# Transposes of the next batch in a fused attention and MLP kernel: one piece moved behind the second half of a product, one piece moved to another ring of accumulation banks

## The chip, the cores and the metric

The kernel runs on one core of one Trainium2 chip. The metric is the device time of one execution in microseconds (us). One execution is also profiled. Before the change the median of three runs was 752.65 us (752.6 to 754.64).

The engines in the profile are PE (TensorE, the matmuls), PEld (its loading of weights, which overlaps PE), DVE (VectorE), ACT (ScalarE) and SP (issues the transfers). In this kernel TensorE's results go to accumulation memory (PSUM), kept as two rings of two banks and a group of four. A tile taken from a ring of two must wait until the tile taken two places earlier has been read out. The granted clock is the share of TensorE's full speed that the profile shows as allowed. The chain that ended last is the work followed back from the last instruction, at each step to what released it.

## The reference, cut to what matters

```python
def _attn_ref(x, state):                    # x (8, 8, 512, 64), state (8, 8, 32, 64)
    scores = scale * x @ state^T            # softmax over the 32 states, then @ state
    scores2 = scale * state @ x^T           # softmax over the 512 tokens, then @ x
    ...
def _moe_ref(x, w_in, w_out):               # 4352 tokens, 512 -> 2048 -> 512
    h = x @ w_in
    g = h * (1.0 / (1.0 + np.exp(-1.702 * h)))
    return (g @ w_out).astype(np.float32)
```

Everything is float32. The kernel computes the second product (`g @ w_out`) by Strassen's method: seven products of blocks, with sums around them, in place of eight. While it does so for batch b, it prepares the attention of batch b+1 in between.

## The kernel before

`att_state` transposes the state of a batch, and `att_xT` transposes one of four pieces of its x. Each writes one bank of ring A (`att_ps`), and ScalarE copies the bank out. Four transposes fill the bank of a piece. Ring H (`psH`) serves other products.

```python
    def att_ps(shape, name):
        return psA.tile(shape, FP32, tag="att", name=name)        # ring A: two banks

    def att_state(b):
        ps = att_ps([P, P], f"stT_{b}")
        nc.tensor.transpose(ps, stn[b].rearrange("p g d -> p (g d)"), ident)
        ...
        nc.scalar.copy(A[b]["stT"], ps)

    def att_xT(b, j):
        ...
        ps = att_ps([P, SCH, P], f"xT_{b}_{j}")
        for c in range(SCH):
            nc.tensor.transpose(ps[:, c], x_heads(b, c, j), ident)
        nc.scalar.copy(A[b]["xT"][:, j], ps.rearrange("p c q -> p (c q)"))
```

The seven products call hooks behind each half. "P1a" is behind the first half of the first product, "P1b" behind its second half and "P2a" behind the first half of the second product. In front of the hooks at P1a runs the tail of the previous stage (`rest`: two short products, each with an addition on VectorE and a gelu on ScalarE, and sums on VectorE).

```python
        at("P1a", att_state, b)
        at("P1a", att_xT, b, 0)
        at("P1a", att_xT, b, 1)
        at("P1b", att_xT, b, 2)
        at("P1b", att_xT, b, 3)
        at("P2a", att_scores, b)
        at("P2a", att_M, b, 0)             # ring A
        at("P2a", att_M, b, 1, True)       # ring H
        ...
        hooks["P1a"] = [(rest, ())] + hooks.get("P1a", [])
```

These hooks run for five batches (3 to 7), while batches 2 to 6 are in their seven products.

Of the kernel before, what the change touches and what calls it, by code (L numbers as in the profile page):

```python
# [10 lines left out]
FP32 = mybir.dt.float32  # L11
# [9 lines left out]
def kernel(  # L21
# [36 lines left out]
    P = 128  # L58
# [3 lines left out]
    SCH = S // P  # L62
# [21 lines left out]
    psH = ctx.enter_context(tc.tile_pool(name="psH", bufs=2, space=bass.MemoryType.PSUM))  # L84
# [4 lines left out]
    def att_ps(shape, name):  # L89
        return psA.tile(shape, FP32, tag="att", name=name)  # L90
# [49 lines left out]
    def x_heads(b, c, j):  # L140
        return xn[b][:, c, NG * j : NG * (j + 1)].rearrange("q g d -> q (g d)")
# [111 lines left out]
        A[b]["stT"] = apool.tile([P, P], FP32, tag="stT", name=f"stT_{b}", bufs=2)  # L253
        nc.scalar.copy(A[b]["stT"], ps)

    def att_xT(b, j):
        if j == 0:
            A[b]["xT"] = apool.tile([P, NPR, S], FP32, tag="xT", name=f"xT_{b}")
        ps = att_ps([P, SCH, P], f"xT_{b}_{j}")
        for c in range(SCH):  # L260
            nc.tensor.transpose(ps[:, c], x_heads(b, c, j), ident)  # L261
        nc.scalar.copy(A[b]["xT"][:, j], ps.rearrange("p c q -> p (c q)"))
# [160 lines left out]
    def att_slots(b):  # L423

        slots = [[] for _ in range(14)]

        def at(i, fn, *args):
            slots[i].append((fn, args))

        at(0, att_state, b)  # L430
        for j in range(NPR):
            at(j, att_xT, b, j)

        at(5, att_scores, b)
        at(5, att_M, b, 0)
        at(5, att_M, b, 1, True)
        at(5, att_blocks, b)
        at(5, att_s_max, b)
        at(5, att_s_exp, b)
        at(5, att_x_exp, b)  # L440
        at(5, att_s_norm, b)
        at(5, att_x_norm, b)
        for g in range(NG):
            at(8, att_eT, b, g)
        at(9, att_sread, b)
        at(9, att_M, b, 3, True)
        at(9, att_M, b, 2)
        at(11, att_srT, b)
        sums_of = up_sums(b)
        for i, fn, args in ((10 if k < 5 else 11 if k < 12 else 12, *v) for k, v in enumerate(sums_of)):  # L450
            at(i, fn, *args)
        return slots
# [288 lines left out]
    def hooks_next(b):  # L741

        h = {}

        def at(name, fn, *args):
            h.setdefault(name, []).append((fn, args))

        at("P1a", att_state, b)
        at("P1a", att_xT, b, 0)
        at("P1a", att_xT, b, 1)  # L750
        at("P1b", att_xT, b, 2)
        at("P1b", att_xT, b, 3)
        at("P2a", att_scores, b)
        at("P2a", att_M, b, 0)
        at("P2a", att_M, b, 1, True)
        at("P2a", att_blocks, b)
        at("P2a", att_s_max, b)
        at("P2a", att_s_exp, b)
        for g in range(NG):
            at("P2a", x_max, b, g)  # L760
            at("P2a", x_sub, b, g)
        at("P2a", x_exp, b)
        at("P2", att_s_norm, b)
        for name, fn, *args in (
            ("P6.1", x_sum, 0), ("P6.2", x_sum, 1), ("P6.3", x_inverse), ("P6.4", x_scale, 0), ("P6.6", x_scale, 1),
        ):
            at(name, fn, b, *args)
        for g in range(NG):
            at("P6", att_eT, b, g)
            at("P6", x_back, b, g)  # L770
        at("P4a", att_sread, b)
        at("P4a", att_M, b, 3, True)
        at("P4a", att_M, b, 2)
        steps = up_sums(b)
        for name, n in (("P4b", 5), ("P7.1", 2), ("P7.2", 1), ("P7.3", 1), ("P7.4", 1), ("P7.6", 1), ("P7", 1), ("P3a", 3)):
            for fn, args in steps[:n]:
                at(name, fn, *args)
            steps = steps[n:]
        assert not steps
        at("P3a", att_srT, b)  # L780
        return h


    def up_sums(b):

        a = A[b]

        def tt(out, x0, x1, op=ALU.subtract):
            nc.vector.tensor_tensor(out=out(), in0=x0(), in1=x1(), op=op)

        def rooms(step):
            if step == 0:
                t = apool.tile([P, NG, NB, Ns], FP32, tag="e1", name=f"ta_{b}").rearrange("p g i n -> p (g i n)")
                a["T"] = [t[:, QT * i : QT * (i + 1)] for i in range(4)]
            elif step == 1:
                t = apool.tile([P, NPR, S], FP32, tag="xT", name=f"ms_{b}")
                a["S1"], a["S2"] = t[:, :2], t[:, 2:]
            else:
                t = apool.tile([P, NG, SCH, P], FP32, tag="eT", name=f"m4_{b}")
                a["S4"] = t.rearrange("p g c q -> p g (c q)")  # L800

        def T(i):
            return lambda: a["T"][i]

        def R(g, i):
            return lambda: a["aT"][:, g, QT * i : QT * (i + 1)]

        def M(c, g):
            return lambda: a["M", c][:, g]

        def V(name, c):
            return lambda: a[name][:, c]

        steps = [(rooms, (0,))]
        steps += [(tt, v) for v in ((T(0), R(0, 1), R(0, 0)), (T(1), R(1, 1), T(0)), (T(2), R(1, 1), R(0, 1)), (T(3), R(1, 0), T(1)))]
        steps.append((rooms, (1,)))
        for c in range(2):
            steps.append((tt, (V("S1", c), M(2 + c, 0), M(2 + c, 1), ALU.add)))
            steps.append((tt, (V("S2", c), V("S1", c), M(c, 0))))
            steps.append((tt, (M(2 + c, 0), M(c, 0), M(2 + c, 0))))  # L820
        steps.append((rooms, (2,)))
        steps += [(tt, (V("S4", c), M(c, 1), V("S2", c))) for c in range(2)]
        return steps
# [248 lines left out]
    for b in range(2, B):  # L1072
        rest = up_strassen(b, S, *parts_x(b))
        if b + 1 < B:
            hooks = hooks_next(b + 1)
        else:

            steps, left, right = sr_sums()
            hooks = {"P3a": steps[9:] + [(low_third, (T2,)), (low_third, (T3,))]}
            for k, name in enumerate(("P1b", "P2a", "P2", "P5a", "P5b", "P6", "P4a", "P4b", "P7")):  # L1080
                hooks[name] = [steps[k]]
        hooks["P1a"] = [(rest, ())] + hooks.get("P1a", [])
        strassen_two(b, out_of(b), hooks)
        if b + 2 < B:
            load_state(b + 2)
            load_x(b + 2)
# [35 lines left out]
```

## Time and profile before

| | before |
|---|---|
| median of runs | 752.65 us |
| span of the profiled run | 750.4 us |
| TensorE busy | 731.6 us, 98% |
| VectorE busy | 501.7 us, 67% |
| ScalarE busy | 232.1 us, 31% |
| TensorE waiting for the copy of the state | 5.3 us in 5 waits |
| granted TensorE clock, mean | 0.998 |

TensorE sets the time, so the rows to look for are those in which TensorE itself stands still. The prediction shows them. One more row is VectorE's first work on the scores of the next batch, from the order of time (start us, length us, engine, line, operation, tiles, shapes, count, and in brackets the idle time before it and what ended it):

```profile
337.52 1.31 DVE L292 STREAM_TRANSPOSE e<-o 128x512 f32<-128x512 f32 x2 [3.19 <-PE o L279]
```

VectorE was idle for 3.19 us before it.

### The profile page before, as it was taken

The page shows a single profiled execution, that of the slowest core. Times are in us where ns is not written, and L with a number is a line of the kernel's source. Part 1 is how long each engine was busy: PE and PEld are TensorE (multiplying, and loading weights), DVE is VectorE, ACT ScalarE, POOL GpSimd, SP SyncE. Part 2 cuts the span into 40 slices and gives each one's busy share as a digit, 9 for nine tenths or more (in the row PEclk, how much of TensorE's full clock was granted, in tenths as well). Part 3 has the DMA queues.
Part 4 walks back from the last instruction along what each step waited for, and adds up shares of the span by engine and source line. Part 5 has one row for each costly group of instructions (what it writes and reads, how often), then busy time and mean ns, then how long its engine had stood idle before and what let it go on. Part 6 is the DMA issues. An engine that isn't in the chain of part 4 may idle for free.

```text
span 750.4 us, 10915 instructions
## 1 busy us (share of the span) xinstructions
PE 731.6 (98%) x4555; PEld 567.4 (76%) x4555; DVE 501.7 (67%) x947; ACT 232.1 (31%) x421; POOL 0.8 (0%) x8
## 2 busy tenths in 40 slices
PE   8989999999999999999999999999999999999996
PEld 3433444467888789878888789878887888899995
DVE  5999799615846775567747666677656774768340
ACT  4676511022324511433134322451143313300220
POOL 0000000000000000000000000000000000000000
PEclk9999999999999999999999999999999999999999
DMA  9811245010030000300040003000030001000000
GB/s 236 331 58 56 93 160 144 0 57 1 29 83 5 1 16 29 74 1 15 2 102 1 15 2 93 10 1 16 29 74 1 15 2 42 1 15 29 15 1 28
DMA packets 48768, 35.29 MB, mean 47 GB/s; under 512 B 36432, under 2 KB 44112, under 8 KB 48720
## 3 DMA queue, kind: packets, MB, share of 16 engines
q1 hardware_dynamic: 48720, 34.61, 16.1%
q8 instruction: 35, 0.57, 0.3%
q14 instruction: 13, 0.11, 0.1%
HBM read 25.69 MB, written 8.91 MB: 46 GB/s over the span
## 4 chain that ended last, share of the span: by engine, by line
PE 94%; SPq 2%; ACT 2%; DMA 1%; DVE 1%; issue 0%; DVEq 0%; ACTq 0%
PE o L645 28%; PE o L890 16%; PE o L522 9%; PE h L461 8%; PE o L479 7%; PE low L597 6%; PE upx L890 6%; PE o L597 4%; PE M L279 4%; PE xT L261 1%; SPq L138 1%; PE sr L410 1%; PE o L279 1%; PE upx_sr L890 1%; DMA out_dram<-osb_sr 1%; PE warm L122 1%
## 5 line engine op out<-in xcount | busy, mean ns | idle before, releaser
L900 DVE TENSOR_TENSOR g<-o,g 128x512 f32<-128x512 f32 (+1 forms) x140 | 88.1, 651 | 87.3 <-PE o L890 86.3
L645 PE MATMUL o<-w_out,g 128*128 128x256 f32 x576 | 130.0, 380 | 0.0
L645 PEld LDWEIGHTS o<-w_out,g 128*128 128x128 f32 x576 | 107.4, 190 | 18.1 <-issue 4.2
L897 ACT ACTIVATE g<-g 128x512 f32<-128x512 f32 (+1 forms) x84 | 49.8, 600 | 100.5 <-DVE g L900 100.5
L890 PE MATMUL o<-ta,M 128*128 128x256 f32 x192 | 49.3, 379 | 0.0
L890 PE MATMUL upx<-aT,M 128*128 128x256 f32 x192 | 49.3, 379 | 0.0
L890 PE MATMUL o<-ta,ms 128*128 128x256 f32 x192 | 48.4, 380 | 0.0
L390 ACT COPY M<-M 128x512 f32<-128x512 f32 x64 | 33.2, 596 | 42.5 <-PE M L279 42.5
L645 PE MATMUL o<-sums,g 128*128 128x256 f32 x192 | 43.8, 382 | 0.0
L522 PE MATMUL o<-w_out,g 128*128 128x256 f32 x192 | 42.9, 380 | 0.0
L645 PE MATMUL o<-sums,later 128*128 128x256 f32 x192 | 42.4, 379 | 0.0
L645 PEld LDWEIGHTS o<-sums,g 128*128 128x128 f32 x192 | 35.6, 190 | 8.6 <-issue 4.2
L522 PEld LDWEIGHTS o<-w_out,g 128*128 128x128 f32 x192 | 36.1, 190 | 6.0 <-issue 1.3
L890 PEld LDWEIGHTS o<-ta,ms 128*128 128x128 f32 x192 | 36.4, 190 | 5.2 <-DVE osb L541 0.3
L890 PEld LDWEIGHTS o<-ta,M 128*128 128x128 f32 x192 | 36.5, 190 | 5.0
L645 PEld LDWEIGHTS o<-sums,later 128*128 128x128 f32 x192 | 36.5, 190 | 5.0
L890 PEld LDWEIGHTS upx<-aT,M 128*128 128x128 f32 x192 | 36.5, 190 | 5.0
L502 DVE TENSOR_TENSOR later<-g,g 128x512 f32<-128x512 f32 (+1 forms) x32 | 20.8, 650 | 21.5 <-ACT g L464 21.5
L279 PE MATMUL M<-w_in,stT 64*32 64x512 f32 x512 | 33.2, 594 | 0.2 <-ACT eT L400 0.2
L461 PE MATMUL h<-low,M 128*128 128x512 f32 x64 | 29.8, 600 | 2.1 <-ACT M L390 2.1
L461 PE MATMUL h<-aT,M 128*128 128x512 f32 x64 | 28.7, 599 | 2.3 <-ACT M L390 2.3
L600 DVE TENSOR_TENSOR pu<-low,pu 128x128 f32<-128x128 f32 x12 | 3.5, 291 | 39.6 <-PE low L597 39.6
(172 smaller groups left out, 1136.6 us busy)
## 6 DMA issues: line engine op xcount, KB each, us to landing
later<-in_moe_w_out_dram SPq DMA_DIRECT2D x16, 512.0 KB
xn<-in_x_dram SPq DMA_DIRECT2D x28, 256.0 KB
w_out<-in_moe_w_in_dram SPq DMA_DIRECT2D x12, 512.0 KB
out_dram<-osb SPq DMA_DIRECT2D x20, 256.0 KB
out_dram<-later SPq DMA_DIRECT2D x12, 256.0 KB
later<-in_moe_w_in_dram SPq DMA_DIRECT2D x4, 512.0 KB
sums<-in_x_dram SPq DMA_DIRECT2D x4, 256.0 KB
stn<-in_state_dram SPq DMA_DIRECT2D x16, 32.0 KB
```

The costliest lines, as they stand in the source:

```text
L122: nc.tensor.matmul(ps, zeros[:, :P], zeros, start=True, stop=True)
L279: nc.tensor.matmul(ps[g][st], A[b]["stT"][rows, st], rhs(rows, j), start=True, stop=True)
L390: nc.scalar.copy(m[:, g], ps[g])
L461: nc.tensor.matmul(hps, lhs[i], rhs[i], start=(i == 0), stop=(i == n - 1))
L479: nc.tensor.matmul(ops, G[key, f // 2][:, f % 2, P * r : P * (r + 1)], w_out[:, f], start=(f == 0), stop=(f == NF - 1))
L502: nc.vector.tensor_tensor(out=s1, in0=a21, in1=a22, op=ALU.add)
L522: nc.tensor.matmul(ps[:, r], lhs[f][:, P * r : P * (r + 1)], rhs[:, f], start=(first and r == 0 and f == 0), stop=(f == HF - 1), skip_grou ...
L597: nc.tensor.matmul(ps, lhs[f], rhs[:, f], start=(f == 0), stop=(f == QF - 1))
L645: nc.tensor.matmul(ps[:, r], lhs[f][:, P * r : P * (r + 1)], rhs[:, f], start=(r == 0 and f == 0), stop=(f == HF - 1), skip_group_check=True,)
L890: nc.tensor.matmul(ps[:, k], lhs[i][:, o : o + P], rhs[i], start=(first and k == 0 and i == 0), stop=(i == n - 1), skip_group_check=True,)
L897: nc.scalar.activation(out=dst, in_=src, func=AF.Gelu_apprx_sigmoid)
L900: nc.vector.tensor_tensor(out=dst, in0=ps, in1=x, op=ALU.add)
```

## The change

The intent is to take out TensorE's wait for the state's copy. Piece 1 moves from P1a to P1b. Piece 3, now the third piece in a row there, takes a bank of ring H.

```diff
-    def att_xT(b, j):
+    def att_xT(b, j, spare=False):
...
-        ps = att_ps([P, SCH, P], f"xT_{b}_{j}")
+        name = f"xT_{b}_{j}"
+        ps = psH.tile([P, SCH, P], FP32, tag="h", name=name) if spare else att_ps([P, SCH, P], name)
...
         at("P1a", att_xT, b, 0)
-        at("P1a", att_xT, b, 1)
+        at("P1b", att_xT, b, 1)
         at("P1b", att_xT, b, 2)
-        at("P1b", att_xT, b, 3)
+        at("P1b", att_xT, b, 3, True)
```

## The prediction

> **What bounds the kernel now.** I read the page first, then who waits for whom on TensorE, then the order of time around each place where the edited function runs. The page's busy line and its chain that ended last say which engine sets the time:
>
> ```profile
> PE 731.6 (98%) x4555; PEld 567.4 (76%) x4555; DVE 501.7 (67%) x947; ACT 232.1 (31%) x421; POOL 0.8 (0%) x8
> ...
> PE 94%; SPq 2%; ACT 2%; DMA 1%; DVE 1%; issue 0%; DVEq 0%; ACTq 0%
> ```
>
> TensorE is busy 731.6 of 750.4 us, and 94% of the chain is its own work, one instruction behind the other. So a microsecond taken from another engine is worth nothing unless TensorE waited for it; what counts is where TensorE stands still. The waits of TensorE alone (total us, times, longest us) name one repeated case:
>
> ```profile
> PE xT L261 <- ACT stT L254: 5.3, 5, 1.1
> PE h L461 <- ACT M L390: 4.4, 3, 2.1
> ```
>
> L261 is the transposes that make xT, exactly the function the change edits; five times they wait for ScalarE's copy of stT. (The second line is in the first two batches, which the change does not touch.) The order of time on TensorE at the second of the five places (start us, length us, engine, line, tiles, count):
>
> ```profile
> 321.00 3.62 PE L645 MATMUL o<-w_out,g 128*128 128x256 f32 x16
> 324.45 1.03 PE L890 MATMUL o<-ta,M 128*128 128x256 f32 x4
> 325.31 1.03 PE L890 MATMUL o<-aT,m 128*128 128x256 f32 x4
> 326.18 0.27 PE L252 MATMUL stT<-ident,stn 128*128 128x128 f32 x1
> 326.29 0.60 PE L261 MATMUL xT<-ident,xn 128*128 128x128 f32 x4
> 327.94 0.65 PE L261 MATMUL xT<-ident,xn 128*128 128x128 f32 x4 [1.05 <-ACT stT L254]
> 328.43 3.62 PE L645 MATMUL o<-w_out,g 128*128 128x256 f32 x16
> 331.89 1.04 PE L261 MATMUL xT<-ident,xn 128*128 128x128 f32 x8
> 332.76 3.62 PE L645 MATMUL o<-w_out,g 128*128 128x256 f32 x16
> ```
>
> The two L645 rows at 321.00 and 328.43 are the first and second half of the first product. Between them stand two short products (L890, the tail of the previous stage), the state's transpose, piece 0 of xT, a hole, and piece 1. Pieces 2 and 3 come after the second half without any hole. ScalarE in the same stretch shows why:
>
> ```profile
> 326.24 0.63 ACT L897 ACTIVATE g<-g 128x512 f32<-128x512 f32 x1 [2.96 <-DVE g L900]
> 327.10 0.63 ACT L897 ACTIVATE g<-g 128x512 f32<-128x512 f32 x1 [0.23 <-DVE g L900]
> 327.64 0.25 ACT L254 COPY stT<-stT 128x128 f32<-128x128 f32 x1
> 327.79 0.59 ACT L262 COPY xT<-xT 128x512 f32<-128x512 f32 x1
> ```
>
> The state goes to one bank of a ring of two (call it A), piece 0 to the other, piece 1 to the first again, so piece 1 needs the state copied out. That copy takes 0.25 us, but it stands in ScalarE's queue behind two gelus, and the second of these waits for VectorE's addition (326.38, 0.69 us) of the last L890 product. The copy ends at 327.89 and piece 1 starts at 327.94.
>
> **What the Trainium skill says.** "Perfetto Trace Analysis", section "Matmuls", wants independent matmul groups to rotate through PSUM banks so that the evacuation of one lies beside the next group's matmuls. Here two banks are too few for three groups in a row, and the trace agrees: the third is the one that waits. "PSUM — Partial Sum Buffer", section "Engine vs sequencer instructions", says that ScalarE's queue is strict FIFO; this trace agrees (the stT copy begins only after both gelus, although its input was ready a microsecond before). "Perfetto Trace Analysis", section "Tensor Engine Instruction (MATMUL, LD_WEIGHTS)", says that the end of a TensorE instruction is an estimate. I therefore count from start to start and not by the idle figure in brackets. This trace shows the need: rows overlap (321.00 + 3.62 is past 324.45).
>
> **The change part by part.** *Number of operations:* nothing is added or removed; per batch 16 xT transposes and four xT copies before and after. Only order and bank change.
>
> *Piece 1 moved behind the second half.* Cost of a transpose where nothing waits: eight in 332.76 − 331.89 = 0.87 us, 0.109 us each. From the state's transpose to the second half TensorE starts 9 transposes; unhindered that is 9 × 0.109 = 0.98 us. The trace has 328.43 − 326.18 = 2.25 us. So the hole costs 2.25 − 0.98 = 1.27 us, a little over the 1.05 in brackets. After the change the state and piece 0 (5 × 0.109 = 0.54 us) are followed at once by the second half: it reads and writes what the first half did (the first product's operands, bank 0 of another group of four) and needs no ring bank. It starts at about 326.73 instead of 328.43, 1.70 us sooner. Piece 1 costs its 0.44 us later, so the net is 1.27 us.
>
> *Does piece 1 wait at its new place?* The second half takes 331.89 − 328.43 = 3.46 us, to about 330.18. The stT copy (done at 327.89) and piece 0's copy (done at 328.38) depend on nothing that moves, so pieces 1 and 2 find both A banks free, by 2.3 and, 0.44 us later, 2.2 us.
>
> *Piece 3 to the other ring (call it H).* Behind the second half there are now three pieces, and with ring A alone piece 3 would need piece 1's copy. That copy begins about 0.64 us after a piece begins (331.89 to 332.53) and takes 0.59, while piece 3 would begin 0.87 us after piece 1; it would wait some 0.4 us. In ring H it takes a bank that the previous stage's products used; their last reader (gelu at 320.33) ended at 320.93, over 10 us earlier. So no wait, and this part preserves the gain rather than adding one.
>
> *What follows.* The matrix M of the next step then uses A and H. Its first two blocks wait for pieces 1 and 2, its next two for an old gelu and for piece 3; all must be copied by the time the scores need xT anyway.
>
> *Sum.* I found the same 1.05 us hole at 246.57, 327.94, 409.31, 490.68 and 572.05, and 2.25 to 2.26 us from start to start from the state transpose to the second half at each (at the last, 570.29 to 572.55). The last batch prepares no next one. So 5 × 1.27 = 6.35 us, 0.84% of 752.65: 746.3 us.
>
> **The rivals.** *One: the wait moves to the scores (L279).* They need all four pieces copied. With the pieces starting at 330.18, 330.62 and 331.05, the three copies end near 331.4, 331.9 and 332.5 by the 0.64 and 0.59 above. The half product after them starts at 331.49 and takes 336.31 − 332.76 = 3.55, so the scores are due at 335.04: 2.5 us to spare. It would need ScalarE to be late by more than that; nothing else is in its queue there but the k1 copy (0.60 us), which comes after the pieces. Were I wrong by all of the margin, the gain would shrink to zero and the time stay at 752.
>
> *Two: VectorE becomes the bound.* It runs from 326.99 without a break to 334.33, on work released by the L890 products, which do not move; then it idles 3.19 us before it transposes the scores at 337.52. Everything after moves 1.27 us closer: 1.92 us of idle time remain. This would cost nothing. For it speaks that VectorE is 67% busy overall; against it that TensorE's waits name VectorE in none of these batches. If its later work were tight, a part of each 1.27 would be given back: two thirds of the gain left would be 748.4.
>
> *Three: only the order changes and the wait was hidden.* Then 752 to 753. Against it: the chain that ended last runs through VectorE's add, the gelu, the stT copy and into piece 1, so this hole is on the path, and TensorE works without a hole from there to the next batch.
>
> *Four: a lower TensorE clock when the pauses go.* The granted clock is 0.998 with TensorE already 98% busy; one more per cent busy should not move it. Half a per cent of clock would cost 3.7 us, 750.
>
> **Range and chances.** The mechanism repeats identically five times and the figure comes from start times, so I expect nearly all of the 6.35 us. Runs of the kernel before lie between 752.6 and 754.64, so the median may shift upwards by a microsecond or so, and up to a third of the gain could be given back: 745.2 to 748.6. More than 6.4 us is hardly possible, as nothing else that the change touches is on the path; a gain of 2% would need 15 us, more than twice all these holes. So same within 2% has nearly all the chance.
>
> **What would show it right or wrong.** In the profile after: the wait of xT for stT on TensorE gone from the list (0 instead of 5.3 us); between the two L645 halves five transposes and no hole, 0.54 us from the state's transpose to the second half; twelve transposes in one row behind it, about 1.31 us to the next half; TensorE's busy time unchanged near 731 us and its share up to about 98.3%; distance between equal points of two batches (81.37 us now, 326.18 to 407.55) down to 80.1. Wrong, if a new wait appears in that row of twelve, or before the scores or M, or if the same holes show up as pauses further on; and if the chain names VectorE more than now, rival two holds.

## The result, and the profile after

The changed kernel took 747.35 us in the median of four runs (745.83 to 748.5), and the kernel before, run on the same chip, took 753.25. The ratio of the two is 0.9918 (95% interval 0.9894 to 0.9942). A ratio here is the mean time of one kernel's runs over that of the other's of the same rounds, so it is not quite the ratio of the medians quoted. The outputs were correct.

The page of the changed kernel, busy line and chain (all lines behind the edit have moved down by one, so L261 is now L262 and L645 is L646):

```profile
PE 732.2 (98%) x4553; PEld 568.0 (76%) x4555; DVE 501.9 (67%) x947; ACT 231.6 (31%) x421; POOL 0.8 (0%) x8
...
PE 95%; SPq 2%; DMA 1%; ACT 1%; issue 0%; DVE 0%; DVEq 0%; ACTq 0%
```

TensorE does the same work in a shorter span: 732.2 of 745.8 us, or 98.2%. In the chain, ScalarE and VectorE have lost one per cent each. The waits of TensorE (total us, times, longest us) begin with:

```profile
PE h L462 <- ACT M L391: 4.4, 3, 2.1
PE warm L122 <- DVE one L113: 1.2, 1, 1.2
PE o L280 <- ACT xT L273: 0.7, 1, 0.7
```

The line that led this list before, xT waiting for stT, is not in it any more. The order of time on TensorE at the same place, the second of five:

```profile
321.53 3.62 PE L646 MATMUL o<-w_out,g 128*128 128x256 f32 x16
324.99 1.03 PE L891 MATMUL o<-ta,M 128*128 128x256 f32 x4
325.85 1.03 PE L891 MATMUL o<-aT,m 128*128 128x256 f32 x4
326.71 0.27 PE L252 MATMUL stT<-ident,stn 128*128 128x128 f32 x1
326.82 0.60 PE L262 MATMUL xT<-ident,xn 128*128 128x128 f32 x4
327.26 3.62 PE L646 MATMUL o<-w_out,g 128*128 128x256 f32 x16
330.71 1.47 PE L262 MATMUL xT<-ident,xn 128*128 128x128 f32 x12
332.02 3.62 PE L646 MATMUL o<-w_out,g 128*128 128x256 f32 x16
```

From the state's transpose to the second half it is now 327.26 - 326.71 = 0.55 us; it was 2.25. The twelve transposes behind the second half take 332.02 - 330.71 = 1.31 us and contain no bracket, hence no wait. The next batch's state transpose starts at 406.81, 80.10 us after this one; before it was 81.37. The chain that ended last, in order of time, confirms it (start us, length us, what; its starts lie up to 0.2 us behind those of the order of time):

```profile
326.88 0.11 PE stT L252
326.99 0.44 PE xT L262 x4
327.42 3.46 PE o L646 x16
330.88 1.31 PE xT L262 x12
```

The chain stays on TensorE. Before, it left TensorE here for VectorE's addition, the gelu and the copy of stT. VectorE's first work on the scores:

```profile
336.78 1.31 DVE L293 STREAM_TRANSPOSE e<-o 128x512 f32<-128x512 f32 x2 [1.92 <-PE o L280]
```

Its idle time fell from 3.19 to 1.92 us, by exactly the 1.27 us that TensorE now comes sooner.

**Why the profiled spans differ by less than 6.35 us.** The two spans differ by 750.4 - 745.8 = 4.6. The rest was lost in the opening, which the change does not touch. The same 16 matmuls in the two profiles, before and after:

```profile
41.91 7.13 PE L461 MATMUL h<-low,M 128*128 128x512 f32 x16 [2.12 <-ACT M L390]
```

```profile
42.03 8.83 PE L462 MATMUL h<-low,M 128*128 128x512 f32 x16 [2.12 <-ACT M L391]
```

They took 1.70 us longer after, with a mean granted clock of 0.91 between 40 and 60 us, where the profile before has 1.00. The wait in front of them is the same 2.12 us in both. Five holes give -6.35, this stretch +1.70 and a later start of it +0.12, which makes -4.5 of the -4.6. Within it the clock is 1.00 until 43.0 us and 0.50 from 43.5 to 46.5. What decides whether this stretch occurs is not shown. Of the eleven profiles with this opening, six have it (the changed kernel and five of the experiments) and five do not (the kernel before, the repeat of the changed kernel and three experiments). The experiment that is as slow as the kernel before has it, and the repeat of the changed kernel has not, so it is not an effect of the change. It goes with much of the spread of the runs of one kernel, as far as the mean clock tells: among the eleven runs of the kernel before in the first group of experiments, the spans lie at 750.7 to 751.6 us where the mean clock was 0.998, and at 752.1 to 753.0 where it was 0.995 or 0.996.

### The profile page after: what moved, and what is told of

It is laid out like the page before. It is cut to its first block, busy times and chain, and to the rows that moved or that the text cites. A ratio compares the mean times of both kernels' runs of the same rounds, so it can differ in the third digit from the quotient of the medians.

```text
span 745.8 us, 10913 instructions
## 1 busy us (share of the span) xinstructions
PE 732.2 (98%) x4553; PEld 568.0 (76%) x4555; DVE 501.9 (67%) x947; ACT 231.6 (31%) x421; POOL 0.8 (0%) x8
## 4 chain that ended last, share of the span: by engine, by line
PE 95%; SPq 2%; DMA 1%; ACT 1%; issue 0%; DVE 0%; DVEq 0%; ACTq 0%
PE o L646 28%; PE o L891 16%; PE o L523 9%; PE h L462 8%; PE o L480 7%; PE low L598 6%; PE upx L891 6%; PE o L598 4%; PE M L280 4%; PE xT L262 2%; SPq L138 1%; PE sr L411 1%; PE o L280 1%; PE upx_sr L891 1%; DMA out_dram<-osb_sr 1%; PE warm L122 1%
## 5 line engine op out<-in xcount | busy, mean ns | idle before, releaser
L646 PE MATMUL o<-w_out,g 128*128 128x256 f32 x576 | 130.0, 380 | 0.0
L646 PEld LDWEIGHTS o<-w_out,g 128*128 128x128 f32 x576 | 107.4, 190 | 18.1 <-issue 4.2
L646 PE MATMUL o<-sums,g 128*128 128x256 f32 x192 | 43.8, 382 | 0.0
L646 PE MATMUL o<-sums,later 128*128 128x256 f32 x192 | 42.4, 379 | 0.0
L646 PEld LDWEIGHTS o<-sums,g 128*128 128x128 f32 x192 | 35.6, 190 | 8.6 <-issue 4.2
L646 PEld LDWEIGHTS o<-sums,later 128*128 128x128 f32 x192 | 36.5, 190 | 5.0
L462 PE MATMUL h<-low,M 128*128 128x512 f32 x64 | 31.5, 630 | 2.1 <-ACT M L391 2.1
```

What stands on the lines that cost most here:

```text
L462: nc.tensor.matmul(hps, lhs[i], rhs[i], start=(i == 0), stop=(i == n - 1))
L646: nc.tensor.matmul(ps[:, r], lhs[f][:, P * r : P * (r + 1)], rhs[:, f], start=(r == 0 and f == 0), stop=(f == HF - 1), skip_group_check=True,)
```

## The experiments

**Theory:** what cost time was the third group in a row needing the bank of the state, whose copy stood behind two gelus in ScalarE's queue. **Rivals:** the order of the work matters in itself; the bank of piece 3 carries a part; the copies or VectorE become the next bound. Every diff is against the changed kernel unless said otherwise. The first four runs shared one chip and eleven runs of the kernel before (median 754.38 us), the next four another group of seven (754.11), the last three these and one more (753.91).

**The changed kernel again** (no edit).

> The changed kernel again, unedited, on the chip of the next three runs, as their mark. Theory (the hole for the state's copy is all that went): 6.35 us below the kernel before, 0.54 us from the state's transpose to the second half product, batches 80.1 us apart. Rival (part of the measured 5.9 us is a luckier or unluckier opening and not the change): a ratio of fast runs clearly away from 0.9916.

Measured: 747.83 us, ratio 0.9917 (0.9903 to 0.9932), batches 80.10 us apart. The result repeats. This run is the mark for the next ones.

**The other ring without the reordering.**

```diff
-        at("P1b", att_xT, b, 1)
+        at("P1a", att_xT, b, 1, True)
         at("P1b", att_xT, b, 2)
-        at("P1b", att_xT, b, 3, True)
+        at("P1b", att_xT, b, 3)
```

> The other ring, but no reordering: piece 1 stays ahead of the second half product as in the kernel before and takes the bank of the other ring; piece 3 goes back to the first ring. Theory (what cost was that the third group in a row needed the state's bank): no hole either, 0.98 us (9 transposes of 0.109) from the state's transpose to the second half, batches 80.1 us apart, time equal to the changed kernel within 0.5 us. Rival (the order matters, because ScalarE needs the time of the half product to clear its queue): a hole of 0.5 us or more stays somewhere, 2.5 us or more above the changed kernel.

Measured: 747.75 us, ratio 0.9911 (0.9896 to 0.9926), batches 80.1 us apart. Its TensorE, in order of time:

```profile
326.92 0.27 PE L252 MATMUL stT<-ident,stn 128*128 128x128 f32 x1
327.03 1.04 PE L262 MATMUL xT<-ident,xn 128*128 128x128 f32 x8
327.90 3.62 PE L646 MATMUL o<-w_out,g 128*128 128x256 f32 x16
```

Pieces 0 and 1 run as one row of eight, and the second half follows after 0.98 us. Piece 1 is where it was in the kernel before, and only its bank is another. So the reordering is not needed. What is needed is that the third group does not take the state's bank before that bank has been read out, and there are two ways to get that.

**The reordering without the other ring.**

```diff
-        at("P1b", att_xT, b, 3, True)
+        at("P1b", att_xT, b, 3)
```

> The reordering without the other ring: three pieces behind the second half, all in the first ring. Theory: the hole for the state goes, but piece 3 waits for piece 1's copy by about 0.4 us (copy ends 0.64 + 0.59 us after piece 1 begins, piece 3 is due 0.87 us after), so batches 80.5 us apart and 5 x 0.4 = 2.0 us above the changed kernel, 4.3 below the kernel before. Rival (the bank change does nothing, the reordering is everything): equal to the changed kernel, no hole in the row of twelve transposes.

Measured: 749.96 us, ratio 0.9943 (0.9929 to 0.9957), which is 2.1 us above the mark; batches 80.56 us apart.

```profile
331.39 1.04 PE L262 MATMUL xT<-ident,xn 128*128 128x128 f32 x8
332.67 0.66 PE L262 MATMUL xT<-ident,xn 128*128 128x128 f32 x4 [0.24 <-ACT xT L263]
333.16 3.62 PE L646 MATMUL o<-w_out,g 128*128 128x256 f32 x16
```

The row of twelve takes 333.16 - 331.39 = 1.77 us instead of 1.31, which is 0.46 more, and five times that is 2.3 us. The bracket shows only 0.24 of it, another case in which start to start tells more than the idle figure. The bank of piece 3 is therefore worth about a third of the whole gain once the pieces stand three in a row.

**The bank of piece 3 without the reordering.**

```diff
-        at("P1b", att_xT, b, 1)
+        at("P1a", att_xT, b, 1)
```

> The other ring for piece 3 without the reordering: piece 1 stays ahead of the second half in the first ring. Theory: the hole for the state is as in the kernel before (1.27 us start to start, five times), batches 81.4 us apart, time equal to the kernel before within 0.5 us. Rival (the bank of piece 3 carries a part of the gain by itself, through the M blocks behind it): 1 us or more below the kernel before.

Measured: 753.62 us, ratio 0.9995 (0.9981 to 1.0009), batches 81.37 us apart. The wait is back as it was:

```profile
PE xT L262 <- ACT stT L254: 5.3, 5, 1.1
```

Alone, the second half of the change does nothing.

**All four pieces in front.**

```diff
-        at("P1b", att_xT, b, 1)
-        at("P1b", att_xT, b, 2)
-        at("P1b", att_xT, b, 3, True)
+        at("P1a", att_xT, b, 1)
+        at("P1a", att_xT, b, 2)
+        at("P1a", att_xT, b, 3)
```

> All four pieces ahead of the second half, all in the first ring: the waits that the change avoids, in a greater dose. Theory (each piece needs the copy of the group two before it): the hole of 1.27 us for the state stays, piece 2 waits next to nothing, piece 3 waits about 0.4 us for piece 1's copy; batches 81.4 + 0.4 = 81.8 us apart, about 2 us above the kernel before. Rival (pieces cost by the switch between products and transposes, not by waits): one row of transposes fewer, so equal to or below the kernel before.

Measured: 755.56 us, ratio 1.0022 (1.0002 to 1.0043), batches 81.82 us apart.

```profile
328.38 1.14 PE L262 MATMUL xT<-ident,xn 128*128 128x128 f32 x8 [1.05 <-ACT stT L254]
329.71 0.66 PE L262 MATMUL xT<-ident,xn 128*128 128x128 f32 x4 [0.19 <-ACT xT L263]
```

Both waits are there, one for the group two before each time. The switches between products and transposes, of which there is one fewer here, gave nothing back.

**Pieces 1 to 3 right before the scores.**

```diff
-        at("P1b", att_xT, b, 1)
-        at("P1b", att_xT, b, 2)
-        at("P1b", att_xT, b, 3, True)
+        at("P2a", att_xT, b, 1)
+        at("P2a", att_xT, b, 2)
+        at("P2a", att_xT, b, 3, True)
```

> Pieces 1 to 3 taken from behind the second half and put right before the scores, so that no product covers their copies (rival one of the prediction, forced). Theory: the scores of pieces 1 to 3 then wait for ScalarE; the last copy ends about 2.34 us after the first of the twelve transposes, its scores are due at about 2.07 us, so a hole of some 0.3 us if the scores wait piece by piece, and of about 1 us if they wait for all pieces at once: 1.5 to 5 us above the changed kernel, with TensorE's wait for the xT copy in the list. Rival (the copies are never near the path, the 2.5 us to spare were not needed): equal to the changed kernel.

Measured: 750.54 us, ratio 0.9963 (0.9938 to 0.9988), batches 80.91 us apart, 0.81 more than the changed kernel, or 4.0 us in five. The list of TensorE's matmul waits does not name it, against what I had expected. It is in the loading of weights for the scores:

```profile
334.99 0.15 PEld L280 LDWEIGHTS o<-xT,stT 64*32 64x32 f32 x8 [0.17 <-issue]
335.35 0.14 PEld L280 LDWEIGHTS o<-xT,stT 64*32 64x32 f32 x4 [0.21 <-ACT xT L263]
335.84 0.11 PEld L280 LDWEIGHTS o<-xT,stT 64*32 64x32 f32 x2 [0.35 <-ACT xT L263]
```

The scores of the later pieces wait for the copy of each piece, 0.21 and 0.35 us. So 0.56 of the 0.81 us is seen as waits. From start to start all of it lies there: from the first scores to the next product it is 338.54 - 334.99 = 3.55 us here and 338.31 - 335.57 = 2.74 in the changed kernel. In the time of the runs, which were on another chip than the mark, it is less: the medians differ by 2.7 us, the ratios by some 3.5. The place behind the second half, with a half product in front of the scores, is what hides the copies.

**More work for VectorE, 8 needless subtractions per batch.**

```diff
+    def extra(n):
+        for _ in range(n):
+            nc.vector.tensor_tensor(out=pu[:, 0], in0=ident, in1=ident, op=ALU.subtract)
...
         at("P1b", att_xT, b, 3, True)
+        at("P1b", extra, 8)
```

> The changed kernel with 8 needless 128x128 subtractions on VectorE per batch (about 0.2 us each, 1.7 us) ahead of its work of the second product (rival two, probed). Theory (1.92 us of idle time remain before VectorE's first work on the scores): no change, within 0.5 us of the changed kernel; the idle time before the transpose of the scores falls to about 0.2 us. Rival (VectorE is the bound in this stretch after the change): each batch 1.7 us longer, 8.5 us above.

Measured: 747.77 us, ratio 0.9916 (0.9901 to 0.9931), batches 80.10 us apart. There is no change, although the dose was larger than planned. One subtraction costs 0.32 us and not 0.2:

```profile
333.12 2.57 DVE L744 TENSOR_TENSOR pu<-ident 128x128 f32<-128x128 f32 x8
```

The whole idle time before the scores was thus used up (the row of the scores' transpose has no bracket any more), and TensorE did not notice.

**The same with 40.** The edit is the same with `extra, 40`.

> The same with 40 subtractions (about 8.4 us per batch), more than the idle time. Theory: VectorE reaches the scores some 6.5 us late; its next idle time, 3.85 us before the first addition of the small products, takes up a part, and the rest, 1 to 3 us a batch, falls on TensorE: 5 to 15 us above the changed kernel, with TensorE waiting for VectorE in the small products. Rival (VectorE has room for it all): no change. Rival (VectorE is the bound): 42 us above.

Measured: 785.09 us, ratio 1.0413 (1.0397 to 1.0429), 37 us above the changed kernel. That is more than twice what I had expected. Two things were mis-sized. The 40 subtractions took 13.02 us, not 8.4. And TensorE was slow after its wait:

```profile
360.68 2.08 PE L598 MATMUL o<-sums,later 128*128 128x128 f32 x8 [4.94 <-DVE osb L653]
362.55 1.91 PE L598 MATMUL low<-low,g 128*128 128x128 f32 x8
364.26 1.92 PE L598 MATMUL low<-sums,later 128*128 128x128 f32 x8
365.97 1.25 PE L598 MATMUL o<-sums,later 128*128 128x128 f32 x8
367.06 1.06 PE L598 MATMUL low<-low,g 128*128 128x128 f32 x8
```

The wait is for VectorE's sum with the second product, which must be read out of its bank before the small products use the bank again. Groups of eight that normally start 0.89 us apart then started 1.87, 1.71 and 1.71 us apart. The granted clock from 360.6 to 366.0 was 0.50. That costs 1.87 + 1.71 + 1.71 - 3 x 0.89 = 2.6 us on top of the pause. The pause itself, from start to start, is 5.11 us and not 4.94: from the product in front (348.67) to the small ones it is 12.01 us, and in the changed kernel 348.77 - 341.87 = 6.90. Together that is 7.7 us; the distance from this batch to the next grew by 7.90 (421.52 - 333.52 = 88.00), and those of the other batches by 6.6 to 7.6. Five of these make the 37 us.

**The same with 20.**

> Half the dose of the run with 40 subtractions, whose size I had misjudged: one takes 0.325 us (13.02 us for 40), so 20 take 6.5 us a batch. With 40, TensorE waited 4.94 us for VectorE's sum with the second product, so VectorE's room up to that sum is 13.02 - 4.94 = 8.1 us. Theory: 6.5 us fit into the room, no change against the changed kernel (within 0.5 us), no wait of TensorE for VectorE. Rival (each late microsecond of VectorE costs TensorE part of it from the first on): 10 us or more above.

Measured: 746.2 us, ratio 0.9903 (0.9884 to 0.9923), batches 80.10 us apart, and no wait of TensorE for VectorE in its list. So VectorE can be 6.5 us late in this stretch without cost. In the changed kernel it has room of about 13.02 - 5.11 = 7.9 us (8.1 with the bracket of 4.94, as expected above).

**The same idea at the opening.** What is left of TensorE's waits is led by the three for M, the same pattern at the start of the program. M of the second batch is computed and needed at once, and its copy stands behind other work in ScalarE's queue. This edit is on top of the changed kernel:

```diff
     up_x(0, 0)
     up_x(0, 1)
-    up_x(0, 2, True)
-    up_x(0, 3, True)
+    att_M(1, 0)
+    up_x(0, 2)
+    up_x(0, 3)
     round_to(NPR + 1)
     att_x_norm(1)
-    att_M(1, 0)
```

> The same idea at the opening, on top of the changed kernel: the block M of the second batch two products sooner, and these two products in the other ring, so that its copy is covered; now TensorE waits 2.12 us for it (3.0 us from end of loading to loading). Theory: TensorE then starts the next products when VectorE's transpose of the same batch is ready, about 2 us sooner: 1.5 to 2.5 us below the changed kernel, and the half-clock stretch behind that pause (1.7 us in some profiles) is gone. Rival (the opening is bound by VectorE's rounding of the weights, so the time comes back at the next M): within 0.5 us of the changed kernel.

Measured: 744.6 us (743.92 to 745.42), ratio 0.9876 (0.986 to 0.9892). This beats the kernel before. The changed kernel did not run in these rounds; the run with 20 subtractions, as fast as it, did, and its four runs (746.06 to 747.76 us) all lie above these.

```profile
40.01 7.42 PE L462 MATMUL h<-low,M 128*128 128x512 f32 x16 [0.31 <-DVE low L343]
```

The wait of 2.12 us for ScalarE has become one of 0.31 us for VectorE's transpose. The state's transpose of batch 2 starts at 161.60 us, against 163.56 in the profile with 20 subtractions: 1.96 us sooner. None of the eight runs of this edit and the next has a mean clock below 0.998, so the half-clock stretch was probably absent from all of them; both profiles are without it.

**And the next M's copy ahead of ScalarE's rounding steps.**

```diff
-    round_to(2 * NPR)
+    round_to(2 * NPR, 2)
     att_M(0, 1)
```

> As the run before, and the copy of the following M ahead of one pair of ScalarE's rounding steps (1.4 us) in ScalarE's queue. Theory: the second pause (1.50 us) shrinks to about 0.3 us, so about 1.2 us below the run before. Rival (VectorE's rounding then waits for the later pair and TensorE for the weights): equal to or above the run before.

Measured: 745.17 us, ratio 0.9885 (0.9871 to 0.99), so no better than the run before. The theory fell. The second wait shrank only from 0.95 to 0.67 us, and a third one, 1.23 us at 58.67, appeared. The state's transpose of batch 2 came 0.49 us later. ScalarE's deferred work stood in front of the next M instead: four pairs of rounding steps between its copies of M at 48.45 and 58.05 us, where the run before has three (49.34 to 57.55).

## Why the prediction was right

**The bound.** TensorE set the time before and after (94% and 95% of the chain), and its busy time did not change. A hole on TensorE was worth its full length: batches 81.37 - 80.10 = 1.27 us shorter, five times, 6.35 us predicted. The two ratios of the changed kernel, 0.9918 and 0.9917, correspond to some 6.2 us.

**Counting from start to start.** The predicted 1.27 us a hole came out to the hundredth. The 1.05 us in the bracket would have predicted batches 1.05 us nearer to each other; they came 1.27 nearer.

**Piece 3.** The estimate of some 0.4 us for its wait without the other ring measured 0.46. The prediction said this part preserves the gain and adds none. The runs with one part each show just that: without the reordering nothing, without the bank 2.1 us less.

**The scores.** I had given the copies 2.5 us to spare. In the profile after, the last of the three copies ends at 332.91 us and the scores begin at 335.57, which is 2.66. With the cover of the half product taken away the loss appears. One sentence of the prediction is wrong here: to be out by all of this margin would have cost nothing, and only what went beyond it would have eaten into the gain.

**VectorE.** The predicted 1.92 us of idle time is the number in the profile. As the basis for "two thirds of the gain left" it was too cautious. The room ahead of the next thing TensorE needs from VectorE is about 7.9 us, since the idle time before the scores is only a part of it.

**The clock.** The rival that a busier TensorE would lose clock did not come true in the stretch that was changed: from 240 to 650 us the granted clock is 1.00 in both profiles. The slower stretch in the opening is there without the change too. It is one reason why the time was 747.35 us and not the predicted 746.3. Another is the starting point: the prediction subtracted from 752.65, and with the fourth run the kernel before has 753.25.

**Which part was the cure.** The prediction named the right cause, the shared bank, but credited the gain to the move of piece 1 alone. The run with only piece 1's bank exchanged shows that the move is one of two ways to the same 80.1 us. That the state's copy was late because of the two gelus in front of it is read from the order of time and was not tested; no run moved the copy in the queue. (Its record begins at 327.64, 0.09 us before that of the second gelu ends, so "only after both" in the prediction holds for the order and not to the tenth.) An estimate from the rows before supports it. Piece 1's last transpose began at about 327.94 + 3 x 0.109 = 328.27, and its copy, with nothing in front, at 328.63, which is 0.36 us later. At that rate the state's copy would have begun at about 326.18 + 0.36 = 326.54, some 1.1 us sooner, and most of the 1.27 us would have gone.

## What to carry to other kernels

When the bound engine repeatedly waits at the third group of a ring of two, look at what stands in front of the reading engine's copy in its queue; the copy itself may take only a small part (here 0.25 us, and the hole was 1.27). Here either a bank from another ring or other work of the bound engine in between removed the wait, and the gain can be counted beforehand as (start to start as it is) minus (instructions times their spacing in an undisturbed row), times the number of places. Check with one run whether the newly crowded place needs a further bank, and look in the opening of the program for the same pattern.

## What the Trainium skill lacked or had wrong

- "TensorE: Matmul & The Clock Gate", section "Part 4: PE-mode transpose", gives about 275 ns for a 128x128 transpose in the context of one kernel, beside a figure for bf16. The records here, in float32, have about the same (272 to 273 ns). But in a row they start 109 ns apart, and that is what a row of transposes costs: 1.31 us for twelve. The section does not give the spacing of transposes.
- The same page, section "What's actually happening", has TensorE fall to half its clock after an idle window of about 3.4 us, and return after about as long a busy one. With a pause of 4.94 us the granted clock indeed fell to 0.50, some 4 us after the pause began; it came back at about 366.3 us, 5.7 us after the matmuls had started again. But in six of eleven profiles the clock also fell in the opening, behind a pause of only 2.12 us (16 matmuls in 8.83 instead of 7.13 us; 0.50 from 43.5 to 46.5 us in the changed kernel, where they start at 42.03). Whether the pause alone does it is not shown, since between the large matmuls on its two sides there were only sixteen matmuls of 64x32 from 38.07 us on. In the two profiles in which the pause is 0.31 and 0.46 us the clock did not fall there.
- "Perfetto Trace Analysis", section "Matmuls", advises to rotate banks so that evacuation overlaps. The section does not say that the depth needed depends on what stands in the evacuating engine's queue. Here a copy of 0.25 us behind two gelus went with a loss of 1.27 us on TensorE.
